# Normalised attention outputs split into high and low parts in PSUM; K's low part on GpSimd; gates applied to transposed reciprocals

## The chip, the core and the metric

The kernel runs on one core of a Trainium2 chip. The metric is the device time of one execution in microseconds (us), taken as the median of several runs. An engine here is one of TensorE (PE, with its weight loader PEld), VectorE (DVE), ScalarE (ACT), GpSimd (POOL) and SyncE (SP, which issues the DMAs). Matrix products land in PSUM, which PE writes and DVE and ACT read and write; POOL works on SBUF alone.

## What is computed

First an attention with pooled queries, 8 batches of 8 heads, then a mixture of four attention experts over its output, two of which are taken for each token:

```python
q_pool = q.reshape(B, H, S // 2, 2, D).mean(axis=3)          # B=8, H=8, S=1152, D=64
scores = scale * (q_pool @ k.transpose(0, 1, 3, 2))
attn = exp(scores - max(scores)); attn = attn / (sum(attn) + 1e-9)
x = (attn @ v), heads side by side                           # [8, 576, 512]
logits = x @ w_gate; topk = the 2 best of 4; w = softmax over them
for e in range(4):
    q, k, v = x @ wq[e], x @ wk[e], x @ wv[e]                # 64 wide each
    a = causal softmax(scale * q @ k.T)
    out += (gate of e, zero where not taken) * (a @ v @ wo[e])
```

All is float32. To keep precision while the matrix engine takes a shorter format (fp32r), each operand is split into a high part and a low part, and products are sums of high*high, low*high and high*low.

## The kernel before

The attention works on 32 pairs of heads (4 per batch, called p), two heads at a time in the upper and lower 64 partitions. For each pair a first pass forms high*high scores and takes row maxima on DVE (`f_max`, 15 steps of two 384-wide reductions into PM). A second pass, `f_st`, forms the transposed scores in 18 steps (two query halves of 288, nine key blocks of 128): eight matmuls into two PSUM banks, the last two of which subtract the row maximum (RM), then two exponentials on ACT into a tile pt. `f_av` multiplies pt with v into a bank acc, and POOL adds pt into sacc, whose column sums give the denominators; the first pt of a half is copied to sacc by ACT.

When a half is done, `g_norm` copies acc to an SBUF tile accs (ACT), sums sacc over its partitions with a matmul of ones into a bank `den`, transposes den in 32x32 blocks into an SBUF tile rd (DVE, L513), adds 1e-9 to the few distinct values in r9 (L517), inverts them (L520) and transposes them back to their full width into rd (L523). `f_xfin` then multiplies accs by rd (DVE, through `any_tt`, which picks DVE or POOL by planned times), writes the high part of x (ACT) and the low part (DVE, accs minus high).

After four pairs a batch's experts run while the next batch's attention goes on: projections (`f_qk`, `f_vproj`, matmuls at L231), the gates on DVE (L646), maxima of causal scores (MPM, L699 and L701), scores, products, and `f_yfin`, which normalises like `f_xfin` and also multiplies by the gates. For that POOL spreads the gate columns over 128 columns (gb, L802), PE transposes each 128-token piece into a bank gp (L807), and DVE multiplies accs by gp. `f_out` multiplies y with wo and writes the result out.

K's tiles arrive by DMA in kraw; ACT casts the high part kh, and `f_prepk` makes the low part kl = kraw - kh, planned for DVE (L255) except at the very start.

PSUM has 8 banks: one for acc, seven in a ring `gen` for everything else. A planner in the kernel's own code (a list of flows, a modelled clock for each engine, due times and costs) writes all engines' instructions in one order; each engine then works its own queue strictly in that order. Helper functions issue the operations, so most instructions carry a helper's line: L231 a plain matmul, L240 a two-head score matmul, L247 a two-head product, L251 an ACT copy or cast, L255 a DVE tensor-tensor, L259 a POOL tensor-tensor.

## Time and profile before

| | before |
|---|---|
| median of 3 runs | 1397.63 us (1393.1 to 1398.59) |
| profiled execution | 1391.8 us, span of its instructions 1390.1 us |
| PE busy | 1327.1 us (95%) |
| DVE busy | 1142.3 us (82%) |
| POOL busy | 921.7 us (66%) |
| ACT busy | 699.6 us (50%) |
| granted TensorE clock | 0.98 of full over the span |

A busy time is the union of an engine's instructions. Matmuls overlap each other in the pipeline and a matmul's end is modelled, so PE's 95% is not PE at its best; who waits for whom has to be read from the waits, the chain and the timeline. Idle time of an engine that is not the bottleneck costs nothing.

### The profile page before, as it was taken

The numbers are of one execution on the slowest core, as the hardware profiler recorded it, in microseconds if no ns is written. First come the engines' busy times: TensorE is split into PE (matmuls) and PEld (weight loads), VectorE is DVE, ScalarE is ACT, GpSimd is POOL, SyncE is SP. The second block draws the span as 40 slices with busy tenths as digits, with TensorE's granted clock in tenths as the row PEclk, the third lists the DMA queues.
The fourth block names the chain that finished last, engine by engine and source line by source line (L and its number), as shares of the span: only waits on it lengthen the run. The fifth ranks groups of instructions, "written<-read, shape, count | busy, mean of one in ns | idle before, by whom it ended". The sixth has DMA issues, their size and how long they took to land.

```text
span 1390.1 us, 30255 instructions
## 1 busy us (share of the span) xinstructions
PE 1327.1 (95%) x11417; PEld 916.7 (66%) x11417; DVE 1142.3 (82%) x2446; ACT 699.6 (50%) x1956; POOL 921.7 (66%) x779
## 2 busy tenths in 40 slices
PE   8999999999999999999999999999999999999988
PEld 5656775667756676657766677566775667756765
DVE  8989798787898888798887978878798787985365
ACT  3556544655455544555445554465544655445523
POOL 3877756866568665785667866577655866577714
PEclk9989999999999999999999999999999999999997
DMA  4221111121111111112011221012110121100001
GB/s 137 70 88 61 52 52 46 32 69 47 53 52 53 58 36 53 47 53 87 7 52 47 68 71 53 24 35 70 63 53 24 41 74 54 53 19 1 17 20 35
DMA packets 40050, 70.36 MB, mean 51 GB/s; under 512 B 4864, under 2 KB 30944, under 8 KB 39904
## 3 DMA queue, kind: packets, MB, share of 16 engines
q1 hardware_dynamic: 39904, 68.43, 15.4%
q8 instruction: 90, 1.47, 0.4%
q14 instruction: 56, 0.46, 0.1%
HBM read 58.73 MB, written 9.44 MB: 49 GB/s over the span
## 4 chain that ended last, share of the span: by engine, by line
PE 63%; DVE 29%; POOL 3%; issue 3%; ACT 2%; DMA 0%; POOLq 0%; SPq 0%; ACTq 0%; DVEq 0%
PE gen L240 27%; PE gen L231 16%; PE acc L247 13%; DVE PM L397 10%; PE gen L247 5%; DVE MPM L701 4%; DVE kl L255 4%; POOL sacc L259 2%; DVE accs L255 2%; DVE gen L699 2%; DVE gate L646 1%; DVE ql L255 1%; DVE rd L513 1%; PE gen L807 1%; ACT pt L460 1%
## 5 line engine op out<-in xcount | busy, mean ns | idle before, releaser
L259 POOL TENSOR_TENSOR sacc<-sacc,pt 128x576 f32<-128x576 f32 (+4 forms) x592 | 849.4, 1437 | 411.3 <-ACT sacc L251 209.6
L460 ACT ACTIVATE pt<-gen 128x288 f32<-128x288 f32 x1152 | 402.4, 414 | 410.0 <-PE gen L240 358.3
L397 DVE TENSOR_REDUCE PM<-gen 128x1 f32<-128x384 f32 (+1 forms) x960 | 471.0, 540 | 107.5 <-PE gen L240 106.2
L247 PE MATMUL acc<-pt,v 128*64 128x288 f32 x2304 | 369.4, 426 | 0.7 <-ACT accs L251 0.2
L240 PE MATMUL gen<-qh,kh 64*128 64x288 f32 x1152 | 231.8, 354 | 26.3 <-DVE PM L397 15.4
L247 PEld LDWEIGHTS acc<-pt,v 128*64 128x64 f32 x2304 | 148.9, 137 | 110.6 <-issue 43.9
L240 PEld LDWEIGHTS gen<-qh,kh 64*128 64x128 f32 x1152 | 125.4, 186 | 136.3 <-DVE PM L397 50.2
L240 PE MATMUL gen<-kh,qh 64*128 64x384 f32 (+1 forms) x960 | 206.1, 385 | 9.5 <-ACT qh L251 6.1
L240 PE MATMUL gen<-qh,kl 64*128 64x288 f32 x1152 | 191.6, 301 | 0.0
L240 PE MATMUL gen<-RM,ON 64*128 64x288 f32 x1152 | 185.1, 295 | 0.0
L240 PE MATMUL gen<-ql,kh 64*128 64x288 f32 x1152 | 184.5, 295 | 0.0
L240 PEld LDWEIGHTS gen<-kh,qh 64*128 64x128 f32 (+1 forms) x960 | 108.6, 179 | 70.5 <-issue 21.4
L240 PEld LDWEIGHTS gen<-RM,ON 64*128 64x128 f32 x1152 | 123.3, 188 | 0.0
L240 PEld LDWEIGHTS gen<-ql,kh 64*128 64x128 f32 x1152 | 122.8, 188 | 0.0
L240 PEld LDWEIGHTS gen<-qh,kl 64*128 64x128 f32 x1152 | 121.0, 188 | 0.0
L255 DVE TENSOR_TENSOR kl<-kraw,kh 128x384 fp32r<-128x384 f32 x93 | 90.6, 974 | 25.4 <-PE gen L240 25.0
L231 PE MATMUL gen<-x,WH 128*128 128x288 f32 (+2 forms) x512 | 108.2, 305 | 1.2 <-DVE MPM L701 1.2
L701 DVE TENSOR_REDUCE MPM<-gen 128x1 f32<-128x128 f32 (+2 forms) x192 | 89.9, 474 | 5.5
L231 PEld LDWEIGHTS gen<-x,WH 128*128 128x128 f32 x512 | 80.7, 188 | 13.0 <-issue 4.0
L231 PE MATMUL gen<-x,WL 128*128 128x288 f32 (+2 forms) x256 | 75.2, 294 | 0.0
L255 DVE TENSOR_TENSOR accs<-accs,rd 128x288 f32<-128x288 f32 (+2 forms) x96 | 72.1, 756 | 2.1
L247 PE MATMUL gen<-sacc,ones 128*64 128x288 f32 (+2 forms) x384 | 65.5, 421 | 4.6 <-POOL sacc L259 3.7
(90 smaller groups left out, 1751.2 us busy)
## 6 DMA issues: line engine op xcount, KB each, us to landing
qraw<-in_qT SPq DMA_DIRECT2D x32, 576.0 KB
kraw<-in_kT SPq DMA_DIRECT2D x96, 192.0 KB
v<-in_vP SPq DMA_DIRECT2D x96, 192.0 KB
out<-ob SPq DMA_DIRECT2D x28, 256.0 KB
wst<-in_wall SPq DMA_DIRECT2D x8, 193.0 KB
out<-pt SPq DMA_DIRECT2D x4, 256.0 KB
RM<-nt SPq DMA_DIRECT2D x62, 2.5 KB
out<-ob SPq DMA_DIRECT2D x7, 128.0 KB
```

The costliest lines, as they stand in the source:

```text
L231: nc.tensor.matmul(o, lhsT, rhs, start=start, stop=stop)
L240: nc.tensor.matmul(o(j), l(HEAD[j]), r(HEAD[j]), start=i == 0, stop=i == len(terms) - 1)
L247: nc.tensor.matmul(o(HEAD[j]), l(j), r(j), start=start, stop=stop)
L255: nc.vector.tensor_tensor(o, a, b, op=op)
L259: nc.gpsimd.tensor_tensor(o, a, b, op=op)
L397: nc.vector.tensor_reduce(pm[:n, j, c, t:t + 1], ps[j][:n, :384], axis=AX.X, op=ALU.max)
L460: nc.scalar.activation(pt[:, j, :HQ], st[j][:, :HQ], AF.Exp, scale=0.0625)
L513: nc.vector.transpose(rd[:, :n], den[:, :n])
L646: f(*a, **kw)
L699: nc.vector.tensor_tensor(ps[j][:m, w - m:w], ps[j][:m, w - m:w], mqk[:m, :m], op=ALU.add)
L701: nc.vector.tensor_reduce(pm[:m, j, c, i:i + 1], ps[j][:m, :w], axis=AX.X, op=ALU.max)
L807: nc.tensor.transpose(gp[:, 128 * t - q0:128 * t - q0 + n], gb[:n].rearrange("p a b -> p (a b)"), ident[:n, :n])
```

## The change

Three things change. First, the reciprocals are transposed back into the PSUM bank `den` instead of rd; the product with accs stays in den, the high part is cast from there by ACT and the low part is den minus high on DVE (`g_split`, used by `f_xfin` and `f_yfin`). The bank is freed after the low part; before, it was freed after the first transpose. The 1e-9 is no longer added on DVE: ACT adds 1e-9/128 to each element of the first pt when it starts sacc. Second, kl is made on POOL for all pairs but the first, due when POOL's modelled backlog is under PLL = 1.5. Third, gb, gp and their transposes go. For each batch four matmuls of the gates with a constant `rep` (sixteen copies of identity blocks, made at the start) put the gates into the layout that the transposed reciprocals have, two DVE copies bring them to a tile gs, and `g_norm` multiplies the 8 or 10 reciprocals of a row by gs before they are transposed back.

```diff
+    for g in range(4):
+        for h in range(4):
+            nc.vector.tensor_copy(rep[:, g, 32 * h:32 * h + 32], ident[:, 32 * g:32 * g + 32])
...
+    def act_first(o, i, n, R, W):
+        nc.scalar.activation(o, i, AF.Copy, bias=1e-9 / 128, scale=1.0)
...
+    def pool():
+        return clk["POOL"] - PLL
...
-        yield lambda: on(3 * p + t in (0, 1) or ("row", 0, 0) in flag, r_kl.avail(), kh.rw, dve())
+        yield lambda: on(3 * p + t in (0, 1) or ("row", 0, 0) in flag, r_kl.avail(), kh.rw, dve() if p == 0 else pool())
         kl = r_kl.new()
-        any_tt(kl.ap, k.ap, kh.ap.bitcast(F32), ALU.subtract, 384, [k, kh], [kl])
+        (any_tt if p == 0 else pool_tt)(kl.ap, k.ap, kh.ap.bitcast(F32), ALU.subtract, 384, [k, kh], [kl])
...
-    def g_norm(acc, sacc, n, box):
+    def g_norm(acc, sacc, n, box, gate=None):
...
-        den.free()
-        yield lambda: rd.w
-        nc.vector.tensor_scalar_add(r9[:, :k], rd[:, :n].rearrange("p (a b) -> p a b", b=32)[:, :, 0], 1e-9)
-        yield lambda: r9.w
-        nc.vector.reciprocal(r9[:, :k], r9[:, :k])
-        yield lambda: r9.w
-        nc.vector.transpose(rd[:, :n].rearrange("p (a b) -> p a b", b=32), r9[:, :k].unsqueeze(2).to_broadcast([128, k, 32]))
+        yield lambda: rd.w
+        o, w = (den[:, 384:384 + k], den) if gate else (r9[:, :k], r9)
+        nc.vector.reciprocal(o, rd[:, :n].rearrange("p (a b) -> p a b", b=32)[:, :, 0])
+        rd.free()
+        if gate:
+            ready, gs, ep, q0 = gate
+            yield lambda: on(ready in flag, gs().rw if ready in flag else 0.0, den.w)
+            nc.vector.tensor_tensor(r9[:, :k], o, gs()[:, ep].rearrange("p t i -> p (t i)")[:, q0 // 32:q0 // 32 + k],
+                                    op=ALU.mult)
+        yield lambda: r9.w
+        nc.vector.transpose(den[:, :n].rearrange("p (a b) -> p a b", b=32), r9[:, :k].unsqueeze(2).to_broadcast([128, k, 32]))
...
+    def g_split(accs, den, n, hi, lo, res):
+        yield lambda: max(den.rw if den.we != "DVE" else den.w, accs.rw)
+        dve_tt(den[:, :n], accs[:, :n], den[:, :n], ALU.mult, n, [accs, den], [den])
+        accs.free()
+        yield lambda: den.rw
+        act_copy(hi, den[:, :n], n, [den], [res])
+        yield lambda: res.rw
+        dve_tt(lo, den[:, :n], hi.bitcast(F32), ALU.subtract, n, [den, res], [res])
+        den.free()
...
+        gs, ps, n = GS[b], r_gen.new(), 4 * nt
+        for i in range(4):
+            nc.tensor.matmul(ps[:, n * i:n * i + n], rep[:, i, :], g, start=True, stop=True)
+        for j in range(2):
+            src = ps[HEAD[j], :4 * n].rearrange("p (i t o e) -> p e o t i", i=4, o=2, e=2)[:, j]
+            nc.vector.tensor_copy(gs[HEAD[j], :, tc_, :], src)
...
-        for t in range(q0 // 128, (q0 + qn + 127) // 128):
-            gs = g[:, t, 2 * ep:2 * ep + 2].unsqueeze(2).to_broadcast([128, 2, 64])
-                nc.gpsimd.tensor_scalar(gb.ap, gs, 1.0, 0.0, op0=ALU.mult, op1=ALU.add)
-            nc.tensor.transpose(gp[:, 128 * t - q0:128 * t - q0 + n], gb[:n].rearrange("p a b -> p (a b)"),
-                                ident[:n, :n])
-        dve_tt(accs[:, :qn], accs[:, :qn], gp[:, :qn], ALU.mult, qn, [accs, gp], [accs])
-        any_tt(accs[:, :qn], accs[:, :qn], rd[:, :qn], ALU.mult, qn, [accs, rd], [accs])
```

Because the planner's times change, all queues are written in a new order. Three places show it. The first is DVE's queue where a batch's expert outputs are normalised, in the fourth batch. Before (PM rows are row maxima, r a ring tile of reciprocals, the 11335 and 11366 gen tiles are gp):

```order
L523 STREAM_TRANSPOSE rd_11350<-r_50_11356 128x320
L397 TENSOR_REDUCE PM_88<-gen_11391 128x1
L397 TENSOR_REDUCE PM_88<-gen_11392 128x1
L255 TENSOR_TENSOR accs_11224<-accs_11224,gen_11335 128x256
L255 TENSOR_TENSOR accs_11224<-accs_11224,rd_11298 128x256
L255 TENSOR_TENSOR kl_11417<-kraw_10702,kh_10780 128x384
L397 TENSOR_REDUCE PM_88<-gen_11421 128x1
L397 TENSOR_REDUCE PM_88<-gen_11422 128x1
L255 TENSOR_TENSOR accs_11245<-accs_11245,gen_11366 128x320
L255 TENSOR_TENSOR accs_11245<-accs_11245,rd_11350 128x320
L513 STREAM_TRANSPOSE rd_11431<-gen_11430 128x288
L255 TENSOR_TENSOR y_11334<-accs_11224,y_11334 128x256
```

After, where L526 is the first transpose, L530 the reciprocal, L536 the product with the gates and L540 the transpose back:

```order
L526 STREAM_TRANSPOSE rd_11167<-gen_11166 128x256
L530 RECIPROCAL gen_11166<-rd_11167 128x8
L536 TENSOR_TENSOR r_50_11185<-gen_11166,gs_11019 128x8
L540 STREAM_TRANSPOSE gen_11166<-r_50_11185 128x256
L265 TENSOR_TENSOR gen_11166<-accs_11156,gen_11166 128x256
L410 TENSOR_REDUCE PM_105<-gen_11247 128x1
L410 TENSOR_REDUCE PM_105<-gen_11248 128x1
L265 TENSOR_TENSOR y_11203<-gen_11166,y_11203 128x256
L526 STREAM_TRANSPOSE rd_11260<-gen_11259 128x320
L530 RECIPROCAL gen_11259<-rd_11260 128x10
L536 TENSOR_TENSOR r_51_11268<-gen_11259,gs_11019 128x10
L540 STREAM_TRANSPOSE gen_11259<-r_51_11268 128x320
```

The products with gp and rd and the kl are gone from between the maxima; one product in the bank, and the low part from the bank, stand there instead, and a gen bank is now named from the first transpose to the row that writes y.

The second is POOL's queue in the third batch, among the sums sacc. Before:

```order
L802 TENSOR_SCALAR gb_9256<-gate_8081 128x128
L259 TENSOR_TENSOR sacc_9200<-sacc_9200,pt_9232 128x2x288
L802 TENSOR_SCALAR gb_9270<-gate_8081 128x128
L259 TENSOR_TENSOR sacc_9200<-sacc_9200,pt_9272 128x2x288
L802 TENSOR_SCALAR gb_9311<-gate_8081 128x128
L259 TENSOR_TENSOR sacc_9200<-sacc_9200,pt_9291 128x2x288
L259 TENSOR_TENSOR sacc_9200<-sacc_9200,pt_9347 128x2x288
L259 TENSOR_TENSOR sacc_9200<-sacc_9200,pt_9371 128x2x288
L259 TENSOR_TENSOR sacc_9200<-sacc_9200,pt_9391 128x2x288
```

After:

```order
L269 TENSOR_TENSOR sacc_8773<-sacc_8773,pt_8804 128x2x288
L269 TENSOR_TENSOR kl_8857<-kraw_8125,kh_8196 128x384
L269 TENSOR_TENSOR sacc_8773<-sacc_8773,pt_8834 128x2x288
L269 TENSOR_TENSOR sacc_8773<-sacc_8773,pt_8861 128x2x288
L782 AFFINE_SELECT pt_8900<-pt_8900 128x2x128
L269 TENSOR_TENSOR sacc_8773<-sacc_8773,pt_8887 128x2x288
L782 AFFINE_SELECT pt_8916<-pt_8916 128x2x128
L269 TENSOR_TENSOR sacc_8783<-sacc_8783,pt_8900 128x640
L269 TENSOR_TENSOR kl_8974<-kraw_8227,kh_8294 128x384
L269 TENSOR_TENSOR sacc_8783<-sacc_8783,pt_8916 128x2x192
L269 TENSOR_TENSOR sacc_8773<-sacc_8773,pt_8944 128x2x288
```

The spread gates gb are gone, and a kl stands after every few sums.

The third is PE's queue in the fourth batch, where the gates are brought to the tokens' columns. Before:

```order
L240 MATMUL gen_11374<-RM_83,ON 128x288
L240 MATMUL gen_11375<-RM_83,ON 128x288
L807 MATMUL gen_11366<-ident,gb_11367 128x128
L240 MATMUL gen_11391<-kh_10708,qh_10509 128x384
L240 MATMUL gen_11392<-kh_10708,qh_10509 128x384
L807 MATMUL gen_11335<-ident,gb_11386 128x128
L807 MATMUL gen_11366<-ident,gb_11389 128x128
L240 MATMUL gen_11404<-qh_9850,kh_9619 128x288
```

After:

```order
L245 MATMUL gen_11001<-RM_100,ON 128x288
L245 MATMUL gen_11002<-RM_100,ON 128x288
L245 MATMUL gen_11013<-kh_10599,qh_10337 128x384
L245 MATMUL gen_11014<-kh_10599,qh_10337 128x384
L706 MATMUL gen_11020<-gate_10495,rep 128x20 x4
L245 MATMUL gen_11028<-mqh_9496,mkh_9549 128x256
L245 MATMUL gen_11029<-mqh_9496,mkh_9549 128x256
```

Single transposes between score matmuls (ten in a batch) are replaced by one group of four 20-column matmuls in each batch.

## Rows read from the trace of the kernel before

**Rows 1.** The page's first part: span; busy us, share, instructions of each engine.

```profile
span 1390.1 us, 30255 instructions
PE 1327.1 (95%) x11417; PEld 916.7 (66%) x11417; DVE 1142.3 (82%) x2446; ACT 699.6 (50%) x1956; POOL 921.7 (66%) x779
```

**Rows 2.** The chain that ended last, whole span: the page's engines; then by line.

```profile
PE 63%; DVE 29%; POOL 3%; issue 3%; ACT 2%; DMA 0%; POOLq 0%; SPq 0%; ACTq 0%; DVEq 0%
...
by line: PE gen L240 26.8%; PE gen L231 16.1%; PE acc L247 13.3%; DVE PM L397 10.2%; PE gen L247 5.5%; DVE MPM L701 3.8%; DVE kl L255 3.5%; issue 2.7%; POOL sacc L259 2.3%; DVE accs L255 1.9%; DVE gen L699 1.7%; DVE gate L646 1.4%; DVE ql L
```

**Rows 3.** Waits, whole span: who waited for whom, us in total, times, longest.

```profile
PE gen L240 <- DVE PM L397: 23.9, 26, 3.1
PE gen L240 <- DVE rd L513: 7.7, 12, 0.8
...
PEld gen L240 <- DVE PM L397: 74.8, 159, 3.4
...
PEld gen L240 <- DVE rd L513: 17.3, 28, 1.1
PEld gen L240 <- DVE MPM L701: 12.3, 24, 1.0
...
PEld gen L240 <- DVE gen L699: 9.6, 25, 0.9
...
ACT pt L460 <- POOL sacc L259: 39.2, 35, 2.0
```

**Rows 4.** Timeline, DVE and PE: start us, us, instruction, [idle before, what ended it].

```profile
4.47 0.76 DVE L255 TENSOR_TENSOR qraw<-qraw 128x576 f32<-128x576 f32 x1 [2.83 <-DMA qraw<-in_qT]
5.50 0.56 DVE L255 TENSOR_TENSOR kl<-kraw,kh 128x384 fp32r<-128x384 f32 x1 [0.28 <-ACT kh L251]
...
235.24 1.75 DVE L255 TENSOR_TENSOR kl<-kraw,kh 128x384 fp32r<-128x384 f32 x1
...
238.60 1.77 DVE L255 TENSOR_TENSOR ql<-qraw,qh 128x576 fp32r<-128x576 f32 x1
...
240.89 0.39 PE L240 MATMUL gen<-qh,kh 64*128 64x288 f32 x1 [0.95 <-DVE PM L397]
```

**Rows 5.** DVE's groups, all shapes together: xcount, busy us, mean ns, idle before.

```profile
L255 DVE TENSOR_TENSOR kl<-kraw,kh 128x384 fp32r<-128x384 f32 x93 | 90.6, 974 | 25.4 <-PE gen L240 25.0 <-ACT kh L251 0.3
...
L255 DVE TENSOR_TENSOR accs<-accs,rd 128x288 f32<-128x288 f32 (+2 forms) x96 | 72.1, 756 | 2.1
L517 DVE TENSOR_SCALAR r<-rd 128x9 f32<-128x9 f32 (+2 forms) x96 | 63.2, 659 | 1.2
L255 DVE TENSOR_TENSOR x<-accs,x 128x288 fp32r<-128x288 f32 x63 | 53.4, 848 | 3.3 <-ACT x L251 3.3
...
L255 DVE TENSOR_TENSOR y<-accs,y 128x256 fp32r<-128x256 f32 (+1 forms) x30 | 29.5, 982 | 2.8 <-ACT y L251 2.8
...
L520 DVE RECIPROCAL r<-r 128x9 f32<-128x9 f32 (+2 forms) x96 | 19.6, 204 | 1.4
L255 DVE TENSOR_TENSOR mql<-gen,mqh 128x288 fp32r<-128x288 f32 (+2 forms) x32 | 14.6, 456 | 26.0 <-ACT mqh L251 25.9
...
L255 DVE TENSOR_TENSOR accs<-accs,gen 128x256 f32<-128x256 f32 (+1 forms) x32 | 14.3, 446 | 11.9 <-PE gen L807 11.8
```

**Rows 6.** POOL's groups, all shapes together.

```profile
L802 POOL TENSOR_SCALAR gb<-gate 128x128 f32<-128x128 f32 x80 | 29.4, 373 | 15.1 <-DVE gate L646 9.7 <-PE gen L807 3.8 <-PE gen L247 1.5
L259 POOL TENSOR_TENSOR kl<-kraw,kh 128x384 fp32r<-128x384 f32 x3 | 3.0, 998 | 3.1 <-ACT kh L251 3.1
```

**Rows 7.** Timeline, PE: two gate transposes, and a wait for a denominators' bank.

```profile
596.02 0.53 PE L807 MATMUL gen<-ident,gb 128*128 128x128 f32 x2
596.49 0.40 PE L240 MATMUL gen<-qh,kh 64*128 64x288 f32 x2
...
601.59 0.41 PE L240 MATMUL gen<-qh,kh 64*128 64x288 f32 x2 [0.76 <-DVE rd L513]
```

**Rows 8.** First four pairs alone: stretch, length, busy us of PE, PEld, DVE, ACT, POOL.

```profile
23.70:149.80 126.10, 119.65 (x1033) 79.52 (x1034) 110.53 (x201) 70.86 (x194) 96.06 (x63) 0.96 0.26 82
```

More of the change, by code (lines that the diff above doesn't have):

```diff
@@ L37 @@
 DV0, DVL, DVT = 1, 1, 0.6
+PLL = 1.5
 SP0, SPL, SPT = 0.3, 0.7, 1.3
 EE0, EES, EET = 0.0, 99, 0
-GBA = 100
 MXA, MXB, MXH, MXL = 1.2, 0.12, 3.9, 4.5
@@ L252, in act_copy @@
         emit("ACT", n / 1200 + (0.05 if psum else 0.083), R, W)
+    def act_first(o, i, n, R, W):
+        nc.scalar.activation(o, i, AF.Copy, bias=1e-9 / 128, scale=1.0)
+        emit("ACT", n / 1200 + 0.083, R, W)
     def dve_tt(o, a, b, op, n, R, W, port=0.0):
@@ L490, in f_av @@
         if c == 0:
-            act_copy(sacc[:, :, :HQ], pt[:, :, :HQ], SQ, [pt], [sacc], False)
+            act_first(sacc[:, :, :HQ], pt[:, :, :HQ], SQ, [pt], [sacc])
         else:
@@ L530, in f_xfin @@
         yield from g_norm(acc, sacc, HQ, box)
-        accs, rd = box
-        yield lambda: rd.rw
+        accs, den = box
         x, xr = X[p], XR[p][hf]
         qc = slice(HQ * hf, HQ * hf + HQ)
-        any_tt(accs[:, :HQ], accs[:, :HQ], rd[:, :HQ], ALU.mult, HQ, [accs, rd], [accs])
-        rd.free()
-        yield lambda: accs.rw
-        act_copy(x[:, 0, qc], accs[:, :HQ], HQ, [accs], [xr], False)
-        yield lambda: xr.rw
-        any_tt(x[:, 1, qc], accs[:, :HQ], x[:, 0, qc].bitcast(F32), ALU.subtract, HQ, [accs, xr], [xr])
-        accs.free()
+        yield from g_split(accs, den, HQ, x[:, 0, qc], x[:, 1, qc], xr)
         flag.add(("x", p, hf))
@@ L678, in f_vproj @@
         op(0.4, tt, g, g, sg.to_broadcast([128, nt, E]), op=ALU.mult)
+        yield (lambda: on(True, r_gen.avail(), gate.rw, r_gs.avail() if b not in GS else 0.0), "C")
+        if b not in GS:
+            GS[b] = r_gs.new()
+        gs, ps, n = GS[b], r_gen.new(), 4 * nt
+        for i in range(4):
+            nc.tensor.matmul(ps[:, n * i:n * i + n], rep[:, i, :], g, start=True, stop=True)
+            emit("PE", 0.2, [gate], [ps])
+        for j in range(2):
+            src = ps[HEAD[j], :4 * n].rearrange("p (i t o e) -> p e o t i", i=4, o=2, e=2)[:, j]
+            nc.vector.tensor_copy(gs[HEAD[j], :, tc_, :], src)
+            emit("DVE", 0.13, [ps], [gs])
+        ps.free()
+        if ts[-1] == 4:
+            gate.free()
         flag.add(("g", b, pt))
@@ L770, in f_mav @@
         if c == 0:
-            act_copy(sacc[:, :, :qn], pt[:, :, :qn], 2 * qn, [pt], [sacc], False)
+            act_first(sacc[:, :, :qn], pt[:, :, :qn], 2 * qn, [pt], [sacc])
         else:
@@ L781, in f_yfin @@
         box = []
-        yield from g_norm(acc, sacc, qn, box)
-        accs, rd = box
-        yield lambda: on(("g", b, qb if b == NB - 1 else 0) in flag)
-        gate = GT[b]
-        g = gate[:, :, 12:16]
+        yield from g_norm(acc, sacc, qn, box, (("g", b, qb if b == NB - 1 else 0), lambda: GS[b], ep, q0))
+        accs, den = box
         if (b, ep) not in Y:
@@ L793, in f_yfin @@
         qc = slice(q0, q0 + qn)
[L794 to L821 removed]
+        yield from g_split(accs, den, qn, y[:, 0, qc], y[:, 1, qc], yr)
         YR[b, ep, qb] = yr
@@ L829, in f_yfin @@
         if all((b, e_, q_) in YR for e_ in range(2) for q_ in range(2)):
-            gate.free()
+            GS[b].free()
             VG[b].free()
```

38 lines of the change are left out of this document (9 added, 29 removed).

## The prediction

> **What bounds the kernel now.** I read the shares of the engines first, then the chain, then the waits, then one wait in the timeline. PE is busy 95% of the span, so at most 63 us of it (1390.1 - 1327.1) are open idle time, and DVE comes next with 82% [rows 1]. The chain that ended last runs over PE for 63% and over DVE for 29% [rows 2]: there are stretches in every batch in which PE's own work does not set the pace. The part of DVE on that chain that this change touches is visible by line: kl 3.5% (48.7 us of 1390.1) and the products into accs 1.9% (26.4 us) [rows 2].
>
> The waits say how that reaches PE. PE's array sat idle 23.9 us for the row maxima and 7.7 us for a denominators' transpose; its weight loader, which also stands still while earlier matmuls finish, sat idle 74.8 + 17.3 + 12.3 + 9.6 = 114.0 us before score matmuls, ended by DVE [rows 3]. In both cases the thing waited for is a gen bank that DVE has not yet read. So DVE costs PE between 32 us (what is open) and 114 us (what ends behind DVE at all).
>
> Why DVE is late shows in one place. At 235.24 a kl took 1.75 us and at 238.60 a ql took 1.77 us, the maxima behind them came late, and PE stood still 0.95 us until 240.89 [rows 4]. The same kl at 5.50, with POOL idle, took 0.56 us [rows 4]. Over the run kl takes 974 ns, products of two SBUF tiles 756 ns, the 9-element addition of 1e-9 659 ns, low parts 848 and 982 ns, while a product with one operand in PSUM takes 446 to 456 ns [rows 5]. DVE operations with both operands in SBUF, and the small addition, are slowed while POOL sums; those with an operand in PSUM are not.
>
> **The change part by part.** Working time is made against the profiled execution, 1391.8 us, which is 5.8 us under the median of 1397.6.
>
> PE's own work. Eighty gate transposes go. Two of them took the place from 596.02 to 596.49, 0.235 us each [rows 7]; alone at a seam they may cost nothing visible, so the ends are 0 and 18.8 us, and I take 18 since most stand alone between score matmuls as in the fence of the change. Thirty-six 20-column matmuls come, in nine groups of four. No row shows such a one; the nearest is the 128-column transpose, 0.235 us, and below it nothing, so 0 to 8.5 us; I take 5, since they stand in groups and four share a bank. Net -13 (ends -19 and +9).
>
> DVE's work. Removed: 92 kl of 974 ns, 89.6 us; the 96 additions, 63.2; the 32 products with gp, 14.3; the 96 products with rd fall from 72.1 to 96 x 456 ns = 43.8, so 28.3; the low parts of x from 53.4 to 64 x 456 ns = 29.2, so 24.2; those of y from 29.5 to 14.6, so 14.9 [rows 5]. That is 234.5 us. Added: 32 small products and 18 copies at the nearest small operation, the reciprocal of 204 ns, 10 us [rows 5]. DVE falls by 224 to about 918 us. The 16 copies of identity blocks lie in the 2.83 us before the first q arrives [rows 4] and cost 0 to 1 us; I take 0.
>
> What of it reaches the end. On the chain 48.7 us of kl go whole; of the accs products 72.1 + 14.3 = 86.4 us become 43.8, so half of 26.4, 13 us. Together 62. The waits bound it by 32 below and 114 above, and the removals alone cannot turn into a loss. The one operation that might get longer is the transpose back, which now writes PSUM and of which no row shows a price: between nothing and one more small operation of 204 ns each, 0 to 20 us of DVE's time, of which about a quarter (62 of 234) would reach the end; I take 0. I take 60, the chain's figure, since it counts only what nothing else covers. What is late next is PE itself and, where DVE still reduces 960 tiles, DVE.
>
> The bank. Den is now held until the low part is written: in DVE's new queue 11 rows stand between, as a median of the 96, and 77 at most; before, it was free after the first transpose. PE already waits for such a bank, 7.7 us in 12 waits, once 0.76 us at 601.59 [rows 3, 7]. Per hold it costs between 0 and 0.76 us, 0 to 73 us in all; the 32 gp banks that go pull the other way. I take +5, near the low end, because a faster DVE shortens all other holds.
>
> The new wait. The product with gs stands in DVE's queue, and the maxima behind it wait with it, and PE for their banks. In seven of eight batches the copies to gs stand 8 or more rows ahead of the first such product, so it finds them done: 0. In the last batch the product of the first 256 tokens stands directly behind the copy and holds two banks meanwhile; 0 to +3 us, I take 0, since the POOL broadcast and PE transposes that went there took as long.
>
> POOL. 92 kl at 998 ns come, 91.8 us; the 80 broadcasts (29.4 us) go [rows 6]. POOL goes from 921.7 to about 981 us with the three low parts that move back to DVE. A kl delays the sums queued behind it by 1 us, those free pt tiles, and ACT waits for pt, 39.2 us now [rows 3]; PE sits behind ACT only when all pt are held. In the new queue a kl stands a median of 27 POOL operations ahead of the scores that use it, so K's low part itself is not late. I take 0, ends 0 and +20. ACT's first copy as an activation and its casts from PSUM stay at the same sizes on an engine that is half idle: 0. No DMA is added or moved past another queue's work that waits for it.
>
> A rule is set against the kl here. By the rows the same subtraction takes 974 ns on DVE and 998 ns on POOL, so nothing is lost by moving it [rows 5, 6]. The Trainium skill (GPSIMD Engine Reference, Engine selection) advises against two-input elementwise work on GpSimd, as about twice slower than VectorE. By that rule kl would be worth half on DVE, about 45 us in place of 89.6, and the 60 above would be about 35; the row decides, as the DVE that the rule compares with is the one of 5.50, not the one beside a busy POOL.
>
> Sum: 1391.8 - 13 - 60 + 5 = 1323.8, and with the 5.8 of the median 1330.
>
> **The rivals.** *PE takes over.* DVE's chain time is replaced at once by PE's, since both are nearly always busy; only the open waits go, 32 us of which perhaps 25, and PE's -13, with +15 for the bank: 1397.6 - 25 - 13 + 15 = 1375. For it speaks PE's 95%; against it that its loader waits 114 us for DVE.
>
> *The bank eats it.* Each of 96 holds costs PE the 0.76 us of 601.59: 1397.6 - 13 - 60 + 73 = 1398, no change. It decides if gen's seven banks are short already; the waits for den so far are only 12. The Trainium skill (PSUM — Partial Sum Buffer, Summary: rules for kernel authors) says "Evacuate promptly", which is this case; the den that is kept through four more steps breaks that rule.
>
> *Everything behind DVE goes.* All 114 us and the -13: 1397.6 - 114 - 13 = 1271.
>
> *POOL becomes the bound, slower than before.* POOL's queue is strict and waits itself for ACT; if its sums pace the pairs, the net 60 us of added work come on top of the span: 1397.6 + 60 - 13 = 1445. It decides where POOL has no idle time to take the kl. The tightest stage is the first four pairs, where POOL works 96.1 of 126.1 us [rows 8]; 12 kl make 108, which still fits, and would bind only below 27 us a pair. So it speaks mostly against it, but it caps the gain there at 18 us.
>
> That the change doesn't do what it says, the operations in PSUM being slower than the 446 to 456 ns, would show as the first rival.
>
> **How the numbers follow.** Forecast 1330, own range 1300 to 1362, 0.60. PE takes over (1362 to 1390) 0.15. Everything goes (under 1300) 0.13. The bank eats it 0.06. POOL, or a slower order for another reason, 0.06. The range of 8 in 10 is 1288 to 1382: the forecast, half of the larger gain and most of the first rival. A measurement of this kernel tells about 0.5% from no change, 7 us. Faster by more than that: 0.60 + 0.13 + 0.14 = 0.87; within: 0.06; slower: 0.07.
>
> **What would show it.** Right: DVE near 920 us and under 70%, x and y low parts near 456 ns, kl on POOL near 1 us, no additions of 1e-9; DVE's share of the chain under 20%; the loader's waits for DVE maxima at half or less; PE's busy time 10 to 15 us less. Wrong: waits of score matmuls that end with a low part of x or y (the bank), ACT waits for sacc over 80 us or POOL over 85% (POOL), or open idle time of PE that stays near 63 us with a DVE that is far less busy (PE's order, or another engine, had set it).

## The result, and the profile after

The changed kernel takes 1362.5 us against 1396.2 us of the kernel before, measured beside it: a ratio of 0.978 with a 95% interval of 0.976 to 0.980. It gained 34 us where the prediction's terms add up to 68. The profiled execution took 1361.4 us, its span 1359.7 us, 30.4 us shorter than before.

The page of the changed kernel, answering to [rows 1]: span; busy us, share and instructions of each engine; then the chain that ended last by engine and by line, answering to [rows 2]. Printed lines have moved: L240 is now L245, L247 is L252, L231 is L236, L397 is L410, L701 is L737.

```profile
span 1359.7 us, 30192 instructions
PE 1314.4 (97%) x11409; PEld 917.9 (68%) x11409; DVE 928.1 (68%) x2295; ACT 701.4 (52%) x1956; POOL 953.8 (70%) x788
...
PE 87%; DVE 8%; DMA 2%; ACT 1%; POOL 1%; issue 1%; SPq 0%; POOLq 0%; DVEq 0%; ACTq 0%
PE gen L245 39%; PE acc L252 22%; PE gen L236 17%; PE gen L252 7%; DVE PM L410 3%; DVE MPM L737 1%; POOL sacc L269 1%; DMA qraw<-in_qT 1%; ACT pt L473 1%; DVE gate L667 1%; PE gen L432 1%; PE gen L706 1%; DVE gen L735 1%; DVE qraw L265 0%; DVE WL L265 0%
```

DVE lost 214 us, PE's busy time 12.7 us, and PE's open idle time went from 63.0 to 45.3 us. The last two make the 30.4 us of the span. The chain went from 63% PE and 29% DVE to 87% and 8%.

The groups of the moved and changed operations (count, busy us, mean ns, idle before), answering to [rows 5, 6]:

```profile
L269 POOL TENSOR_TENSOR kl<-kraw,kh 128x384 fp32r<-128x384 f32 x95 | 96.1, 1013 | 41.7 <-PE gen L245 36.0 <-ACT kh L256 5.6
L540 DVE STREAM_TRANSPOSE gen<-r 128x288 f32<-128x288 f32 (+2 forms) x96 | 46.3, 483 | 3.3
...
L265 DVE TENSOR_TENSOR gen<-accs,gen 128x288 f32<-128x288 f32 (+2 forms) x96 | 43.7, 456 | 2.0
...
L265 DVE TENSOR_TENSOR x<-gen,x 128x288 fp32r<-128x288 f32 x64 | 28.6, 448 | 10.9 <-ACT x L256 10.9
...
L265 DVE TENSOR_TENSOR y<-gen,y 128x256 fp32r<-128x256 f32 (+1 forms) x32 | 14.5, 452 | 17.3 <-ACT y L256 16.2
...
L536 DVE TENSOR_TENSOR r<-gen,gs 128x8 f32<-128x8 f32 (+1 forms) x32 | 5.1, 160 | 0.6
...
L706 PE MATMUL gen<-gate,rep 128*128 128x20 f32 (+2 forms) x72 | 9.6, 267 | 0.0
```

DVE's and POOL's durations are near where the prediction put them: products and low parts with an operand in PSUM take 448 to 456 ns, K's low part 1013 ns on POOL, the transpose into PSUM 483 ns (468 ns into SBUF before), the new small product 160 ns. PE's new small matmuls are the exception: 36 in the code stand as 72 in the trace and take 9.6 us, where the prediction had 5.

The waits of PE and of its loader (us in total, times, longest), and ACT's for POOL, answering to [rows 3]:

```profile
PE gen L245 <- DVE MPM L737: 6.9, 10, 0.8
...
PE gen L245 <- DVE PM L410: 6.1, 8, 1.5
```

```profile
PEld gen L245 <- DVE PM L410: 51.3, 143, 1.8
...
PEld gen L245 <- DVE MPM L737: 17.4, 39, 1.0
...
PEld gen L245 <- DVE gen L735: 8.8, 20, 0.4
...
PEld gen L432 <- DVE y L265: 3.4, 7, 0.5
...
PEld gen L245 <- DVE gen L540: 2.6, 6, 0.4
PEld gen L245 <- DVE gen L265: 2.6, 6, 0.4
```

```profile
ACT pt L473 <- POOL sacc L269: 13.2, 13, 1.6
```

PE's open wait for maxima fell from 23.9 to 6.1 us. The loader's four waits behind DVE were 114.0 us; three of the kinds are still listed, with 77.5 us. Those that end with one of DVE's steps on a bank that holds den or its split are the last three rows of the second fence, 8.6 us, and with the smaller rows 12.5 us, where the first transpose of den alone was 17.3 [rows 3]. Of these only 3.8 us end with a low part, the step that frees the bank, and 0.4 us of that is before a score matmul. ACT waits for POOL's sums 13.2 us in place of 39.2.

By stage, each kernel's span cut at the start of the fifth pair and at the last score step (length; then busy us of PE, loader, DVE, ACT, POOL; granted clock). First the kernel before, then the changed one:

```profile
0.00:149.80 149.80, 137.19 (x1076) 89.28 (x1078) 130.15 (x250) 75.94 (x202) 103.85 (x79) 0.97 0.28 88
149.80:1312.50 1162.70, 1123.63 (x9896) 779.45 (x9894) 966.64 (x2059) 597.77 (x1683) 788.72 (x661) 0.99 0.15 48
1312.50:1390.10 77.60, 66.26 (x455) 47.96 (x451) 45.47 (x138) 25.85 (x71) 29.12 (x41) 0.90 0.07 25
```

```profile
0.00:142.50 142.50, 130.66 (x1038) 86.13 (x1038) 111.69 (x241) 74.38 (x198) 109.86 (x89) 0.98 0.27 88
142.50:1295.70 1153.20, 1132.37 (x10016) 796.05 (x10015) 787.86 (x1946) 606.33 (x1700) 827.40 (x679) 0.99 0.15 49
1295.70:1359.70 64.00, 51.42 (x360) 35.76 (x358) 28.57 (x108) 20.70 (x58) 16.56 (x22) 0.92 0.06 20
```

In the long middle DVE works 179 us less and the stretch is only 9.5 us shorter. The tail is 13.6 us shorter, in part because some of PE's work of it now lies ahead of the last score step: the tail has 95 fewer of PE's instructions, the middle 120 more. So the question is why so little of DVE's relief arrived.

### The profile page after: what moved, and what is told of

It reads as the page before. It is cut to its first block, busy times and chain, and to the rows that moved or that the text cites. A ratio compares the mean times of both kernels' runs of the same rounds, so it can differ in the third digit from the quotient of the medians.

```text
span 1359.7 us, 30192 instructions
## 1 busy us (share of the span) xinstructions
PE 1314.4 (97%) x11409; PEld 917.9 (68%) x11409; DVE 928.1 (68%) x2295; ACT 701.4 (52%) x1956; POOL 953.8 (70%) x788
## 4 chain that ended last, share of the span: by engine, by line
PE 87%; DVE 8%; DMA 2%; ACT 1%; POOL 1%; issue 1%; SPq 0%; POOLq 0%; DVEq 0%; ACTq 0%
PE gen L245 39%; PE acc L252 22%; PE gen L236 17%; PE gen L252 7%; DVE PM L410 3%; DVE MPM L737 1%; POOL sacc L269 1%; DMA qraw<-in_qT 1%; ACT pt L473 1%; DVE gate L667 1%; PE gen L432 1%; PE gen L706 1%; DVE gen L735 1%; DVE qraw L265 0%; DVE WL L265 0%
## 5 line engine op out<-in xcount | busy, mean ns | idle before, releaser
L269 POOL TENSOR_TENSOR sacc<-sacc,pt 128x576 f32<-128x576 f32 (+4 forms) x592 | 824.0, 1395 | 329.2 <-ACT sacc L261 186.4
L410 DVE TENSOR_REDUCE PM<-gen 128x1 f32<-128x384 f32 (+1 forms) x960 | 475.8, 546 | 182.9 <-PE gen L245 181.1
L252 PE MATMUL acc<-pt,v 128*64 128x288 f32 x2304 | 369.0, 426 | 3.0 <-ACT pt L473 2.8
L245 PE MATMUL gen<-qh,kh 64*128 64x288 f32 x1152 | 225.5, 356 | 7.8 <-DVE PM L410 4.6
L252 PEld LDWEIGHTS acc<-pt,v 128*64 128x64 f32 x2304 | 150.7, 137 | 115.5 <-issue 40.0
L245 PE MATMUL gen<-kh,qh 64*128 64x384 f32 (+1 forms) x960 | 196.4, 383 | 11.4 <-ACT qh L256 6.2
L245 PEld LDWEIGHTS gen<-qh,kh 64*128 64x128 f32 x1152 | 123.7, 186 | 119.8 <-issue 51.6
L245 PE MATMUL gen<-qh,kl 64*128 64x288 f32 x1152 | 187.5, 299 | 0.0
L245 PE MATMUL gen<-RM,ON 64*128 64x288 f32 x1152 | 182.5, 295 | 0.0
L245 PE MATMUL gen<-ql,kh 64*128 64x288 f32 x1152 | 182.2, 294 | 0.0
L245 PEld LDWEIGHTS gen<-kh,qh 64*128 64x128 f32 (+1 forms) x960 | 104.3, 182 | 66.4 <-issue 31.0
L269 POOL TENSOR_TENSOR kl<-kraw,kh 128x384 fp32r<-128x384 f32 x95 | 96.1, 1013 | 41.7 <-PE gen L245 36.0
L245 PEld LDWEIGHTS gen<-RM,ON 64*128 64x128 f32 x1152 | 120.9, 188 | 0.0
L245 PEld LDWEIGHTS gen<-ql,kh 64*128 64x128 f32 x1152 | 120.6, 188 | 0.0
L245 PEld LDWEIGHTS gen<-qh,kl 64*128 64x128 f32 x1152 | 119.2, 189 | 0.0
L236 PE MATMUL gen<-x,WH 128*128 128x288 f32 (+2 forms) x512 | 108.4, 305 | 2.3 <-DVE PM L410 1.4
L737 DVE TENSOR_REDUCE MPM<-gen 128x1 f32<-128x128 f32 (+2 forms) x192 | 90.1, 476 | 14.1 <-PE gen L245 8.6
L236 PEld LDWEIGHTS gen<-x,WH 128*128 128x128 f32 x512 | 80.9, 188 | 12.3 <-issue 5.6
L526 DVE STREAM_TRANSPOSE rd<-gen 128x288 f32<-128x288 f32 (+2 forms) x96 | 46.0, 479 | 61.3 <-PE gen L252 59.3
L236 PE MATMUL gen<-x,WL 128*128 128x288 f32 (+2 forms) x256 | 75.3, 294 | 0.0
L765 ACT ACTIVATE pt<-gen 128x320 f32<-128x320 f32 (+4 forms) x224 | 62.9, 380 | 18.8 <-PE gen L245 18.5
```

Source lines behind the costliest of these rows:

```text
L236: nc.tensor.matmul(o, lhsT, rhs, start=start, stop=stop)
L245: nc.tensor.matmul(o(j), l(HEAD[j]), r(HEAD[j]), start=i == 0, stop=i == len(terms) - 1)
L252: nc.tensor.matmul(o(HEAD[j]), l(j), r(j), start=start, stop=stop)
L269: nc.gpsimd.tensor_tensor(o, a, b, op=op)
L410: nc.vector.tensor_reduce(pm[:n, j, c, t:t + 1], ps[j][:n, :384], axis=AX.X, op=ALU.max)
L526: nc.vector.transpose(rd[:, :n], den[:, :n])
```

## Experiments: how much can each engine give

The first theory (A) was the rival *PE takes over*: DVE's time on the chain lies beside PE's work, and only PE's open waits go. Against it stood B: the 60 us were there, and a new cost (the bank, POOL, the order) took them back. To tell them apart, DVE or PE was made cheaper in both kernels with the order of the instructions that remain kept: either each row maximum reads a third of its columns, or the high-by-low product of the scores is left out.

```diff
-                nc.vector.tensor_reduce(pm[:n, j, c, t:t + 1], ps[j][:n, :384], axis=AX.X, op=ALU.max)
+                nc.vector.tensor_reduce(pm[:n, j, c, t:t + 1], ps[j][:n, :128], axis=AX.X, op=ALU.max)
```

**Before, maxima thinned.** 

> The kernel before, order of every engine's instructions unchanged, but each of the 960 row-maximum reductions reads 128 of its 384 columns (so the maxima are those of a third of the keys). DVE loses about 256 us (256 columns less at 0.96 columns a ns, 960 times), more than the change took from it (214). Theory A (PE's own work lies beside the DVE time on the chain, and only the 41 us that PE stood open for DVE can go): 1355 to 1376 us. Theory B (the 60 us were there to be had, and the changed kernel lost half of them again to a new cost: the bank den held longer, POOL's additional work, or a poorer order): 1336 us or less.

Measured: 1366.2 us against 1395.9 (ratio 0.979, 0.977 to 0.982).

**Changed, maxima thinned.** 

> The changed kernel with the same thinning: each row-maximum reduction reads 128 of 384 columns, order unchanged, DVE about 256 us less. Theory A: only what is left of PE's open waits for DVE goes, at most 21 us: 1340 to 1357 us. Theory B: with DVE this idle den is held more briefly too, so if the bank took the gain back it is returned here: 1335 us or less; if POOL took it, no change, 1357 to 1365.

Measured: 1336.2 us (0.957 of before, 0.955 to 0.959), 26 us under the changed kernel.

The kernel before, thinned: the page's engines, the chain by engine, and three groups of DVE.

```profile
PE 1298.6 (95%) x11417; PEld 906.0 (66%) x11417; DVE 940.2 (69%) x2446; ACT 698.2 (51%) x1956; POOL 918.7 (67%) x779
...
PE 81%; DVE 11%; POOL 4%; ACT 2%; issue 1%; DMA 1%; POOLq 0%; SPq 0%; ACTq 0%; DVEq 0%
```

```profile
L397 DVE TENSOR_REDUCE PM<-gen 128x1 f32<-128x128 f32 (+1 forms) x960 | 225.2, 278 | 187.3 <-PE gen L240 184.3
...
L517 DVE TENSOR_SCALAR r<-rd 128x9 f32<-128x9 f32 (+2 forms) x96 | 80.7, 840 | 1.2
L255 DVE TENSOR_TENSOR accs<-accs,rd 128x288 f32<-128x288 f32 (+2 forms) x96 | 80.5, 844 | 2.1
```

A DVE as idle as the changed kernel's (940 us against 928) brings 30 us in the order of before, in which nothing else was touched: nearly what the whole change brings. Two things show in the rows. PE's busy time fell by 28.5 us although it carries out the same instructions in the same order at the same mean granted clock (0.982 in both), so "busy" held waiting that the profile does not show as idle. And DVE's busy time fell by 202 us while the maxima alone fell by 246: the additions of 1e-9 went from 659 to 840 ns [rows 5] and the products with rd from 756 to 844, so part of a relief on DVE goes into operations that POOL slows. That POOL slows them shows in the trace of the kernel before: the 13 additions beside which no sum of POOL ran took 159 ns on average, the other 83 took 737 ns.

The left-out product is one of four pairs of matmuls of each of the 576 score steps; a pair starts 0.13 us after the one before it, as in the rows of 600.74 and 600.87 in the last section, so about 75 us in all, an estimate.

```diff
-            for j in range(2):
+            for j in range(2) if i != skip else ():
                 nc.tensor.matmul(o(j), l(HEAD[j]), r(HEAD[j]), start=i == 0, stop=i == len(terms) - 1)
...
-                      [kh, kl, qh, ql, rm], st)
+                      [kh, kl, qh, ql, rm], st, 2)
```

**Before, without high-by-low.** 

> The kernel before without the high-by-low product of the attention scores (one of the four pairs of matmuls of each of the 576 score steps is left out, about 0.13 us a pair, 75 us of PE's time); the planner still counts them. Theory A: PE paces it, but DVE is 82% busy and becomes the next bound, so half or more comes through: 1335 to 1360 us. Theory B (DVE's chain time sets the pace in much of the span): less than 25 us comes through, 1372 us or more.

Measured: 1385.5 us (0.993, 0.990 to 0.995), 10 us less.

**Changed, without high-by-low.** 

> The changed kernel with the same 75 us of PE's work left out. Theory A: PE alone paces it, so most comes through, 55 to 75 us: 1288 to 1307 us, and it falls further than the kernel before does. Theory B (a held bank or POOL paces it): less than 30 us comes through, 1332 us or more.

Measured: 1314.7 us (0.942, 0.937 to 0.946), 48 us under the changed kernel.

The kernel before without the product: engines and chain.

```profile
PE 1287.5 (93%) x10265; PEld 855.4 (62%) x10265; DVE 1131.1 (82%) x2446; ACT 696.1 (50%) x1956; POOL 922.4 (67%) x779
...
PE 55%; DVE 34%; POOL 6%; issue 3%; ACT 2%; DMA 0%; POOLq 0%; SPq 0%; DVEq 0%; ACTq 0%
```

Of 75 us of PE's work, 10 come through before the change and 48 after it. Neither theory holds for all four runs. In the kernel before, the thinned run is in A's range and the one without the product in B's; both runs of the changed kernel lie between the two ranges. So theory A was wrong about the kernel before: PE alone does not set its pace. With a cheap DVE it goes to 1366, with a cheap PE to 1386; both floors lie within 30 us of 1396, and relief of either engine meets the other at once. In the changed kernel PE's work counts for most of what it takes, and thinned maxima still bring 26 us.

## Experiments: each part alone

**K's low part on POOL, alone, in the kernel before.**

```diff
+        yield lambda: on(3 * p + t in (0, 1) or ("row", 0, 0) in flag, r_kl.avail(), kh.rw, dve() if p == 0 else pool())
...
+        (any_tt if p == 0 else pool_tt)(kl.ap, k.ap, kh.ap.bitcast(F32), ALU.subtract, 384, [k, kh], [kl])
```

> The kernel before with one part of the change: K's low part on POOL for all pairs but the first. DVE -90 us, POOL +92 us. After the thinning and the left-out product the theory is now that the kernel before sits between two floors that lie close together, one of DVE's order (1385 us with 75 us less of PE's work) and one of PE's (1366 us with 256 us less of DVE's). Theory A (a part of the DVE relief comes through at about a tenth, as it did for the thinning: 30 us from 256): 9 us from the 90, so 1380 to 1392 us. Theory B (the chain's 48.7 us of kl are real and the bank ate the gain of the whole): 1355 us or less. Theory C (POOL's added work costs as much as DVE saves): 1393 us or more.

Measured: 1425.7 us against 1391.4 (ratio 1.024, 1.021 to 1.026).

**The split in PSUM alone** (den kept, product and low part there, 1e-9 folded into ACT's first copy).

```diff
+        dve_tt(den[:, :n], accs[:, :n], den[:, :n], ALU.mult, n, [accs, den], [den])
...
+        act_copy(hi, den[:, :n], n, [den], [res])
...
+        dve_tt(lo, den[:, :n], hi.bitcast(F32), ALU.subtract, n, [den, res], [res])
```

> The kernel before with one part of the change: den stays in its PSUM bank, is multiplied and split there, and the addition of 1e-9 is folded into ACT's first copy of pt; the gates stay as before (broadcasts, transposes and a product with gp). DVE about -130 us. Theory A (a tenth to a fifth of the DVE relief comes through, the held bank costs nothing): 1370 to 1385 us. Theory B (the bank held longer takes the relief back): 1393 us or more.

Measured: 1430.2 us (1.028, 1.026 to 1.031).

**The gates alone.**

```diff
+            nc.vector.tensor_tensor(r9[:, :k], r9[:, :k], gs()[:, ep].rearrange("p t i -> p (t i)")[:, q0 // 32:q0 // 32 + k],
+                                    op=ALU.mult)
```

> The kernel before with one part of the change: the gates, laid by small matmuls and multiplied into the transposed reciprocals; K's low part on DVE and the splits in SBUF as before. PE -18 us of transposes and +5 of small matmuls, DVE about -5, POOL -29; the last batch loses the chain over POOL, PE and ACT to the gated products. Theory A: PE's 13 us count little in the middle, where DVE's order also paces (75 us of PE brought 10), but the last batch's tail gets shorter: 6 to 16 us, 1380 to 1390 us. Theory B (PE paces throughout): 13 us and the tail's, 1365 to 1377 us.

Measured: 1389.6 us (0.999, 0.997 to 1.000). DVE's busy time rose by 20 us, to 1162.3, where 5 less were expected.

**The whole change, K's low part back on DVE.**

```diff
-        (any_tt if p == 0 else pool_tt)(kl.ap, k.ap, kh.ap.bitcast(F32), ALU.subtract, 384, [k, kh], [kl])
+        any_tt(kl.ap, k.ap, kh.ap.bitcast(F32), ALU.subtract, 384, [k, kh], [kl])
```

> The changed kernel with K's low part back on DVE. DVE +90 us, POOL -92 us. Theory A (PE paces now, a tenth of DVE's 90 us comes through): 1366 to 1376 us. Theory B (kl's chain time is whole, and something else hides it): 1385 us or more. Theory C (POOL's 92 us are what took the gain): 1355 us or less.

Measured: 1414.2 us (1.017, 1.015 to 1.018), 52 us above the changed kernel.

Two parts with which DVE falls by 50 and 115 us (1092.8 and 1027.2 us in their pages) make the kernel slower by 34 and 39 us, the third changes nothing, and together they gain 34. The parts do not add up. The first two fell into the ranges that blame POOL's added work and the held bank. But in each of these kernels the planner also made a new order from the changed work: with K's low part on POOL, about 2870 lines of difference on PE's 8565 rows, and with the gates alone about 1780. So a part's price and its order's price were mixed, and the next runs separate them for K's low part; for the split and for the gates they stay mixed.

## Experiments: the same order, and another order for the same work

In three kernels the planner is told the old engine and cost while the subtraction runs on the other engine, so that the orders of PE, ACT and SP stay (but for 6 rows of PE in two of them). The fourth has the order of the part alone with the work of before.

**Order of before, K's low part on POOL.**

```diff
+            nc.gpsimd.tensor_tensor(kl.ap, k.ap, kh.ap.bitcast(F32), op=ALU.subtract)
+            emit("DVE", 384 / 960 + 0.069 + PORT, [k, kh], [kl])
```

> The kernel before with K's low part on POOL for all pairs but the first, but with the planner told that it still runs on DVE at DVE's cost: the order of PE, ACT and SP stays that of the kernel before (6 rows of 8565 moved on PE). DVE -90 us, POOL +92 us. Theory O (the 34 us that this part alone lost came from the planner's new order): a tenth of the DVE relief comes through, 1380 to 1393 us. Theory E (they are the price of POOL's added work): 1410 us or more.

Measured: 1395.3 us against 1394.0 (ratio 1.000, 0.999 to 1.002).

**Order of the part alone, K's low part on DVE.**

```diff
+            nc.vector.tensor_tensor(kl.ap, k.ap, kh.ap.bitcast(F32), op=ALU.subtract)
+            emit("POOL", 384 * 0.0023 + 0.06, [k, kh], [kl])
```

> The counterpart: the order that the planner makes for K's low part on POOL in the kernel before (the order of the run that took 1425.7 us), with the subtraction still carried out on DVE. The amount of work of every engine is that of the kernel before; only the order differs. Theory O: 1420 to 1445 us. Theory E: 1400 us or less.

Measured: 1431.5 us (1.027, 1.024 to 1.030).

**Order of the changed kernel, K's low part on DVE** (the same two lines, in the changed kernel).

> The changed kernel, order of PE, ACT and SP unchanged, with K's low part carried out on DVE at the place where the planner put it on POOL. DVE +90 us, POOL -92 us. Theory O: a tenth to a quarter of the 90 us, 1366 to 1385 us, and the rest of the 52 us that came with the planner's own order for this is the order's. Theory E: 1400 us or more.

Measured: 1405.0 us (1.008, 1.005 to 1.010), 43 us above the changed kernel.

**Order of before, K's low part on POOL and no additions of 1e-9.**

```diff
+            nc.gpsimd.tensor_tensor(kl.ap, k.ap, kh.ap.bitcast(F32), op=ALU.subtract)
...
-        nc.vector.tensor_scalar_add(r9[:, :k], rd[:, :n].rearrange("p (a b) -> p a b", b=32)[:, :, 0], 1e-9)
...
-            act_copy(sacc[:, :, :HQ], pt[:, :, :HQ], SQ, [pt], [sacc], False)
+            act_first(sacc[:, :, :HQ], pt[:, :, :HQ], SQ, [pt], [sacc])
```

> The kernel before, order of PE, ACT and SP kept (6 rows of PE moved), with K's low part on POOL and the 96 additions of 1e-9 gone (ACT's first copy of pt adds it instead). DVE -153 us, POOL +92 us. Theory A (a tenth to a fifth of the DVE relief comes through until PE paces, floor 1366 us as in the thinning): 1368 to 1382 us. The recorded step (the share of the chain comes through whole, here 48.7 us for K's low part and whatever the chain has of the additions): 1347 us or less. Theory E (POOL's added work takes the gain): 1395 us or more.

Measured: 1387.3 us (0.995, 0.993 to 0.996), 7 us less, between the ranges of theories A and E.

In the kernel before, the move of K's low part itself is worth nothing (0 in its own order, 6 us in the other), and the order that the planner makes for it costs 37 us. In the changed kernel the same move is worth 43 us in an order that is kept and 52 with a new one, so the expectation that only a tenth to a quarter of it would show there was wrong: what it is worth depends on the other two parts, or on the orders that were made with them.

What stands in its way in the kernel before is read from the fourth kernel, in which the additions are gone too: the chain by engine and by line, and two waits for the gates' broadcasts, the first with its row in the kernel before (L802 and L807 there are L810 and L815 here).

```profile
PE 62%; POOL 23%; DVE 7%; issue 4%; ACT 3%; DMA 0%; POOLq 0%; SPq 0%; ACTq 0%
PE gen L240 26%; POOL sacc L264 18%; PE gen L231 16%; PE acc L247 16%; PE gen L247 3%; ACT pt L469 2%; DVE gate L654 2%; POOL kl L383 2%; DVE MPM L709 2%; POOL pt L754 2%; DVE PM L406 1%; PE gen L815 1%; POOL gb L810 1%; DVE gen L707 1%; ACT sacc L256 1%
```

```profile
PE gen L807 <- POOL gb L802: 0.6, 2, 0.4
```

```profile
PE gen L815 <- POOL gb L810: 8.3, 13, 1.1
```

```profile
PEld gen L815 <- POOL gb L810: 22.0, 35, 1.6
```

DVE's share of the chain fell from 29% to 7%, and POOL's rose from 3% to 23%: the sums behind K's low parts, and the broadcasts that PE waits for, 0.6 us of open wait before and 8.3 now. In the changed kernel these broadcasts are gone and POOL is 1% of the chain. That the new gates are what makes POOL's room was not tried by itself.

The last question was how much of all this is the order. Both kernels, their work untouched, were given two other orders by a change in the planner's costs alone:

```diff
-                emit("DVE", 0.465, [ps[j]], [pm])
+                emit("DVE", 0.54, [ps[j]], [pm])
```

**Before, first other order.** 

> The kernel before, the work of every engine unchanged; the planner is told that a row maximum costs 0.54 us (as the trace has it) in place of 0.465, so it makes another order (3662 lines of difference on PE's 8565 rows). Theory O (the orders of both kernels are singled out by their constants): 1415 to 1440 us. Theory W (the gain is the work's and another order costs little): 1380 to 1410 us.

Measured: 1432.9 us against 1394.1 (1.028, 1.027 to 1.030).

**Changed, first other order.** 

> The changed kernel with the same other cost of a row maximum (2470 lines of difference on PE). Theory O: 1385 to 1420 us, and the distance to the kernel before under the same cost may be anything from 0 to 50. Theory W: 1350 to 1375 us, with 25 to 45 us between the two kernels.

Measured: 1361.3 us (0.977, 0.976 to 0.979).

```diff
-SWITCH = 0.1
+SWITCH = 0.12
```

**Before, second other order.** 

> The kernel before, the work unchanged; the planner is told that a change between kinds of matmuls costs PE 0.12 us in place of 0.1 (3338 lines of difference on PE). Theory O: 1415 to 1440 us. Theory W: 1380 to 1410 us.

Measured: 1434.6 us (1.029, 1.027 to 1.031).

**Changed, second other order.** 

> The changed kernel with the same other cost of a change between kinds of matmuls (2260 lines of difference on PE). Theory O: 1385 to 1420 us. Theory W: 1350 to 1375 us, with 25 to 45 us between the two kernels.

Measured: 1374.1 us (0.986, 0.984 to 0.987).

The kernel before is singled out: three other orders for its work take 1431 to 1435 us, 37 to 41 more than its own. The changed kernel moves by -1 and +12. So theory O came true before the change, and of theory W the small price of another order after it, but not its 25 to 45 us between the kernels: 72 and 61 us lie between the two in the other orders, and 34 in their own. Not every new order costs the kernel before so much: with the gates alone it also had one, and took 1390 us.

Are those 40 us DVE's time, which the order of before hides? The maxima were thinned in the two other orders of before, each order kept.

**First other order, thinned.** 

> The kernel before in the first other order (1432.9 us), order kept, with each row-maximum reduction reading 128 of its 384 columns (maxima of a third of the keys), DVE about 256 us less. Theory H (before's own order saves its 40 us by hiding DVE's time; in another order the same relief brings more): 1360 to 1380 us, 53 to 73 us less. Theory S (the other order loses its 40 us to waits that have nothing to do with DVE): as in before's own order 20 to 35 us less, 1398 to 1413 us.

Measured: 1391.8 us against 1395.3 (0.998, 0.996 to 1.000), 41 us under the same order unthinned.

**Second other order, thinned.** 

> The same in the second other order (1434.6 us): each row-maximum reduction reads 128 of 384 columns, order kept. Theory H: 1360 to 1382 us. Theory S: 1399 to 1415 us.

Measured: 1370.4 us (0.983, 0.979 to 0.987), 64 us less.

In its own order the relief brought 30 us, here 41 and 64. In the second order the excess is DVE's nearly whole (34 of 40 us, within theory H's range). In the first it is so in small part (11 of 39 us, between the two ranges); PE's waits there stay with POOL. The first other order, unthinned and then thinned:

```profile
PE gen L807 <- POOL gb L802: 15.4, 20, 1.4
PE gen L240 <- DVE PM L397: 12.5, 24, 1.6
PE gen L247 <- POOL sacc L259: 7.7, 13, 2.6
```

```profile
PE gen L247 <- POOL sacc L259: 16.4, 24, 2.9
PE gen L807 <- POOL gb L802: 13.3, 19, 1.6
...
PE gen L240 <- DVE PM L397: 3.7, 10, 0.4
```

The wait for maxima goes from 12.5 to 3.7 us, but that for the broadcasts stays at 13.3 and that for the sums doubles.

## Why the prediction was right on the parts and wrong on the gain

**Right: the size of the parts.** DVE 928 us (forecast 918), low parts and products at their PSUM price, K's low part at 1013 ns, POOL 954 (981). PE's busy time moved by -12.7 (-13), which is partly luck: the gate transposes that went had taken 23.5 us, not 18, the small matmuls that came take 9.6 us, not 5, and the thinned run moved PE's busy time by 28.5 us with no work taken from it.

**Right: the bank.** The loader's waits that end with a step on den or its split are 8.6 us, 12.5 with the smaller rows, against 17.3, and PE's open ones, 7.7 us, are gone from the list [rows 3]. *The bank eats it* did not happen, and the +5 us of the sum do not show. The Trainium skill (PSUM — Partial Sum Buffer, Summary: rules for kernel authors) asks to evacuate promptly; the trace of the changed kernel shows no price for holding the bank longer. In the split alone PE stood 7.2 us open for x's low parts, but that is a small part of that kernel's 39 us, and its order was not held, so the bank's price there stays open.

**Wrong: "What of it reaches the end".** This step took 60 us, the chain's figure, "since it counts only what nothing else covers". It does not. K's low part had 48.7 us of the chain and was to go whole; moved alone in the order of before it brought 0 (interval -2 to +3 us). All of it with the additions brought 7, and in the trace of that run POOL's sums and broadcasts have taken DVE's place on the chain. A relief of DVE as large as the change's, with nothing moved elsewhere, brought 30. The chain is one path through a kernel in which two or three engines are late by nearly the same amount; its share says what ended last, not how far behind the next one is. The two floors, 1366 with a cheap DVE and 1386 with a cheap PE, say that, and the chain does not show them. The term of 60, set beside the runs, is 18 of open idle time in the profile and about 30 by the thinned run. One of the prediction's own signs failed with it: the loader's waits for maxima were to fall to half or less, and fell from 74.8 to 51.3 us.

**Also wrong: the bound below it.** The open waits for DVE, 32 us, were taken as what DVE relief is sure to bring, and only 18 us of open idle went. The 63 us of PE's idle time were not the most that could go, either: with PE's work unchanged its busy time shrank by 28.5 us in the thinned kernel. The Trainium skill (Perfetto Trace Analysis, Identifying the Most-Contended Engine) calls matmul busy time a poor measure of how near TensorE is to its limit; the traces agree, with PE 95% busy before and in the thinned run and 28.5 us between them.

**What was not in it: the order's price.** The prediction read the new order for single places and gave its whole a mention in one rival of 0.06. For the same work the order alone makes 37 to 41 us before and -1 to 12 after, more than any term of the sum but the 60. In the two other orders the change brings 61 and 72 us, the size of the forecast's 68; but the kernel before as it stands has an order that is worth about 40 us to it, and the changed kernel has none that is worth as much in the orders tried. That the order of before hides DVE's time is shown against the second order; against the first it is the smaller part, and the rest stays open.

**The rivals.** *PE takes over* gave 1375, 13 us above the measured time, and was nearest in kind: PE is 87% of the chain, and in the changed kernel 48 of 75 us of PE's work come through. It is not whole, since thinned maxima still bring 26 us. *Everything behind DVE goes* did not happen: 1336 us needs the maxima thinned as well. *POOL becomes the bound* did not happen in the changed kernel, where POOL is 1% of the chain; with K's low part moved in the order of before its share rose to 23%, with no loss of time. Its first four pairs got shorter by 7.3 us, under the cap of 18, with POOL the tightest beside PE there.

**The rule on GpSimd.** The Trainium skill (GPSIMD Engine Reference, Engine selection) would have halved what K's low part is worth. The row of 1013 ns on POOL against 974 on DVE [rows 5] does not agree with that rule here; what the move was worth went by its company: 0 beside the old gates and splits, 43 us beside the new ones.

**Open.** Why the changed kernel is less sensitive to its order was not tried; that it is because DVE now idles 32% of the span is argued only. Which of the three parts makes the 34 us is open too, since the split and the gates were not tried in a held order. Whether a better order exists for it is open too: the two others were not faster.

## What to carry to other kernels

A share of the chain says what ended last, not how far behind the next engine is; before taking it as a gain, make one engine cheap in place, with the order kept, and see where the floor of the others lies. Where a planner sets the order, a part tried alone is tried together with a new order: hold the order (tell the planner the old cost) to price the part, and perturb the planner on both sides to price the order, before believing that parts add up or that a part is bad. PE's busy share is no measure of its work when its instructions are queued behind one another; compare the busy time of the same instructions in two runs.
